# Attention feeding a feed-forward layer on one core: float16 operand parts under power-of-two scales in place of float32r parts

## The chip, the core and the metric

The kernel runs on one core of a Trainium2 chip. The metric is the device time of one execution in microseconds (us). Three timed runs of the kernel before gave 1097.66, 1099.0 and 1102.61 us: a median of 1099.0 us.

The core has five engines that each work through their own list of instructions in order: TensorE (PE, with its weight loads shown as PEld), VectorE (DVE), ScalarE (ACT), GpSimd (POOL) and SyncE (SP, which here issues the DMAs).

## What is computed

Random-feature attention over 8 batches and 8 heads (576 tokens, 64 dimensions, 128 features), and behind it a feed-forward layer on all 4608 tokens (512 to 2048 to 512, with a gelu). `setup_inputs` multiplies q by 4.675.

```python
def phi(x):                       # x = q * D**-0.25 or k * D**-0.25
    h = einsum('bhsd,md->bhsm', x, omega) - sum(x * x) / 2
    return exp(h - max(h)) / sqrt(m)
kv  = einsum('bhsm,bhsd->bhmd', phi(k), v);  z = sum(phi(k), axis=2)
out = einsum('bhsm,bhmd->bhsd', phi(q), kv) / (einsum('bhsm,bhm->bhs', phi(q), z) + 1e-06)
x   = out.transpose(0, 2, 1, 3).reshape(4608, 512)
h   = x @ w_in                    # 4608x512 @ 512x2048
g   = 0.5 * h * (1 + erf(h / sqrt(2)))
y   = g @ w_out                   # 4608x2048 @ 2048x512, float32
```

The two weight matrices arrive as float64; the kernel reads them as pairs of 32-bit words and makes float32 of them on the chip.

## The kernel before

**Attention** is cut into 32 units (a batch and a pair of heads). The first 4 units run ahead of everything else, in plain float32; the next 4 run in plain float32 beside the feed-forward work; the last 24 use split operands: a value is rounded to a high part, the rest is the low part, and the product is summed from high x high, high x low and low x high. A unit's result is written, transposed and divided, into tiles `xs[n, j]` of 128 x 384 values (`div`).

**The feed-forward layer** is cut into 12 blocks `n` of 384 tokens and 16 chunks `c` of 128 hidden columns. For each chunk `mm1` (L613) makes h from 4 pieces `j` of x and w_in, with 3 matmuls each (12 of 384 columns, L622); `act_high` (L624) applies the gelu to g and rounds it to `gh`; `act_low` (L633) makes `gl` = g - gh; `mm2` (L638) adds the chunk's share to the outputs of the block's three groups of 128 tokens, 3 matmuls each (9 of 512 columns, L645 to L647). All operands of these matmuls are float32r. `block_high` (L601) and `block_low` (L608) split a block's x in the same way on ACT and DVE (on POOL in block 0).

**Weights** come in 32 pieces of 128 x 512 (16 of w_in, 16 of w_out). For each, ACT scales the words (`w_scale`), DVE joins their bits (`w_bits`, L136 and L137), POOL adds the low word (`w_round`, L141), one of DVE, ACT or POOL rounds the high part (`w_high`, L148 to L152), and DVE (w_out) or POOL (w_in) subtracts for the low part (`w_low`, L155). A piece can go through all its steps as soon as it has landed.

**Order.** Every step is put into one list of events with a due time (`at(t, fn, ...)`, in steps of which a chunk of the feed-forward layer takes `SUB` = 6), the list is sorted, and the engines' instruction lists come from it; a scheduling layer below may still move instructions of one engine past each other. Attention units are spread over the feed-forward chunks by the list `bursts`. So PE's list interleaves chunks with attention matmuls, and an engine that waits holds all that stands behind it.

## Time and profile before

| | |
|---|---|
| timed runs | 1097.66, 1099.0, 1102.61 us (median 1099.0) |
| the profiled execution | 1100.79 us |
| its span, first to last instruction | 1098.9 us |
| mean granted TensorE clock | 0.992 |
| start to the first feed-forward matmul | 54.5 us |
| block 0 | 54.5 to 182.0 us |
| blocks 1 and 2 | 182.0 to 350.8 us |
| blocks 3 to 9 | 350.8 to 957.5 us |
| blocks 10 and 11 (no attention left) | 957.5 to 1098.9 us |

A block is counted from the first of its `mm1` matmuls to the first of the next block's. The span is what the profile covers, 1.9 us less than the execution's own time. In a row of the timeline the columns are the start in us, the duration in us, the engine, the line, the operation, the tiles (out<-in), the shape and how many were merged into the row; in square brackets stands an idle time before it and what ended it. In a group's row the numbers behind the bar are the busy time in us and the mean of one in ns, and then the idle time before them. The end of a matmul is modelled, and neighbours overlap; how fast matmuls follow each other is read from their starts. The rows themselves stand in the prediction.

### The profile page before, as it was taken

The page shows a single profiled execution, that of the slowest core. Times are in us where ns is not written, and L with a number is a line of the kernel's source. Part 1 is how long each engine was busy: PE and PEld are TensorE (multiplying, and loading weights), DVE is VectorE, ACT ScalarE, POOL GpSimd, SP SyncE. Part 2 cuts the span into 40 slices and gives each one's busy share as a digit, 9 for nine tenths or more (in the row PEclk, how much of TensorE's full clock was granted, in tenths as well). Part 3 has the DMA queues.
Part 4 walks back from the last instruction along what each step waited for, and adds up shares of the span by engine and source line. Part 5 has one row for each costly group of instructions (what it writes and reads, how often), then busy time and mean ns, then how long its engine had stood idle before and what let it go on. Part 6 is the DMA issues. An engine that isn't in the chain of part 4 may idle for free.

```text
span 1098.9 us, 17294 instructions
## 1 busy us (share of the span) xinstructions
PE 1049.1 (95%) x6022; PEld 906.3 (82%) x6022; DVE 789.7 (72%) x1780; ACT 618.0 (56%) x1310; POOL 482.4 (44%) x554
## 2 busy tenths in 40 slices
...
GB/s 232 169 110 150 164 117 60 70 44 44 75 44 56 84 56 52 62 50 47 72 56 56 75 32 56 57 62 55 56 74 41 49 63 1 1 29 1 30 1 30
DMA packets 46279, 70.92 MB, mean 65 GB/s; under 512 B 13680, under 2 KB 22256, under 8 KB 46192
## 3 DMA queue, kind: packets, MB, share of 16 engines
...
q14 instruction: 39, 0.32, 0.1%
...
## 4 chain that ended last, share of the span: by engine, by line
PE 64%; DVE 18%; ACT 2%; issue 2%; POOL 1%; POOLq 0%; ACTq 0%; DVEq 0%
PE h L622 27%; PE acc L647 9%; PE acc L646 9%; PE acc L645 9%; PE at L468 3%; PE at L400 3%; DVE gl L635 2%; DVE et L285 2%; PE at L249 2%; DVE mx L287 2%; PE at L277 1%; DVE xs L497 1%; DVE rt L485 1%; DVE rc L486 1%; DVE rt L488 1%
## 5 line engine op out<-in xcount | busy, mean ns | idle before, releaser
L622 PE MATMUL h<-xh,wih 128*128 128x384 f32 x768 | 263.2, 343 | 0.0
L622 PE MATMUL h<-xl,wih 128*128 128x384 f32 x768 | 262.5, 342 | 0.0
L622 PE MATMUL h<-xh,wil 128*128 128x384 f32 x768 | 262.0, 341 | 0.0
L645 PE MATMUL acc<-woh,gh 128*128 128x512 f32 (+1 forms) x576 | 230.8, 401 | 0.0
L647 PE MATMUL acc<-wol,gh 128*128 128x512 f32 (+1 forms) x576 | 226.6, 393 | 0.0
L646 PE MATMUL acc<-woh,gl 128*128 128x512 f32 (+1 forms) x576 | 226.2, 393 | 0.0
L635 DVE TENSOR_TENSOR gl<-g,gh 128x384 fp32r<-128x384 f32 x192 | 128.6, 670 | 121.1 <-ACT gh L630 120.6
L242 POOL TENSOR_TENSOR r<-xt,r 64x256 fp32r<-64x256 f32 (+2 forms) x216 | 173.8, 813 | 59.5 <-ACT r L236 46.4
L629 ACT ACTIVATE g<-h 128x384 f32<-128x384 f32 x192 | 94.4, 491 | 170.0 <-PE h L622 161.0
L373 POOL TENSOR_SCALAR kh<-et 128x256 f16<-128x256 f32 (+1 forms) x120 | 50.2, 425 | 280.8 <-ACT et L320 176.0
L622 PEld LDWEIGHTS h<-xh,wih 128*128 128x128 f32 x768 | 145.1, 189 | 7.7 <-issue 1.8
L622 PEld LDWEIGHTS h<-xh,wil 128*128 128x128 f32 x768 | 145.0, 189 | 6.3 <-issue 0.9
L622 PEld LDWEIGHTS h<-xl,wih 128*128 128x128 f32 x768 | 145.3, 189 | 1.3 <-issue 0.9
L647 PEld LDWEIGHTS acc<-wol,gh 128*128 128x128 f32 x576 | 108.3, 188 | 23.9
L645 PEld LDWEIGHTS acc<-woh,gh 128*128 128x128 f32 x576 | 108.5, 188 | 14.6 <-issue 1.5
L646 PEld LDWEIGHTS acc<-woh,gl 128*128 128x128 f32 x576 | 108.6, 189 | 12.8 <-issue 0.4
L236 ACT CAST r<-xt 128x256 fp32r<-128x256 f32 (+2 forms) x216 | 88.2, 410 | 51.9 <-PE at L277 44.2
L630 ACT CAST gh<-g 128x384 fp32r<-128x384 f32 x192 | 98.8, 515 | 3.3
L381 DVE SCALAR_TENSOR_TENSOR kl<-et,kh 128x256 f16<-128x256 f32 (+1 forms) x120 | 65.2, 559 | 30.7 <-POOL kh L373 28.9
L327 DVE STREAM_TRANSPOSE qt<-et 128x288 f32<-128x288 f32 x96 | 45.2, 471 | 51.8 <-ACT et L320 51.4
L141 POOL TENSOR_TENSOR wb<-wb,raw 128x512 int32<-128x512 int32 x32 | 44.0, 1376 | 67.5 <-DVE wb L137 30.3
L254 ACT COPY lo<-at 128x256 f32<-128x256 f32 (+1 forms) x120 | 41.9, 349 | 55.4 <-PE at L249 53.5
...
## 6 DMA issues: line engine op xcount, KB each, us to landing
...
```

Source lines behind the costliest of these rows:

```text
L236: nc.scalar.copy(u.r[i][:, 0:b - a], xf[:, a:b])
L242: nc.gpsimd.tensor_tensor(r, xf[D:, a:b], r, op=ALU.subtract)
L327: nc.vector.transpose(u.qt[g], ef[:, slice(*XG[NK + g])])
L373: nc.gpsimd.tensor_scalar(kh[:, :n], es, KSC, 1.0, op0=ALU.mult, op1=ALU.mult)
L381: nc.vector.scalar_tensor_tensor(kl[:, :n], es, KSC, kh[:, :n], op0=ALU.mult, op1=ALU.subtract)
L622: nc.tensor.matmul(h[:, 0:T], w, (xh, xh, xl)[k], start=(i == 0), stop=(i == 3 * NJ - 1))
L629: nc.scalar.activation(g, h[:, 0:T], AF.Gelu)
L630: nc.scalar.copy(gh, g)
L635: nc.vector.tensor_tensor(gl, g, gh, op=ALU.subtract)
L645: nc.tensor.matmul(acc, gh[:, s], woh[:, c, c0:c1], start=(c == 0), stop=False)
L646: nc.tensor.matmul(acc, gl[:, s], woh[:, c, c0:c1], start=False, stop=False)
L647: nc.tensor.matmul(acc, gh[:, s], wol[:, c, c0:c1], start=False, stop=(c == NF - 1))
```

## The change

- The four weight tiles are float16 in place of float32r. The joined float32 weights are kept for the whole run in a new tile, `w32`.
- **A scale for each weight matrix, found on the chip.** When a piece has been joined, DVE takes its largest absolute value (`w_max`). When all 16 pieces of a matrix have one, a *chain* of small steps makes a scale of them: DVE takes the maximum over the pieces (`chain_a`), PE transposes the 128 values (`chain_b`), DVE takes their maximum (`chain_c`), PE spreads it over the partitions by a matmul with ones (`chain_d`), DVE keeps the exponent bits (`chain_e`), and POOL makes from them a power of two and its inverse (`chain_f`, three instructions). Only then can `w_high` and `w_low` run: so they are put behind the chains, for w_in from due time 72 and for w_out from 91, within block 0, and no longer piece by piece. `w_high` is on POOL and ACT in turn, `w_low` on DVE for all 32 pieces.
- **A scale for each block of x** from block 1 on, by the same chain: four maxima of 128 x 384 on DVE (`block_max`), the chain, and three more POOL instructions (`block_scales`); `block_high`, `block_low`, the gelu, `gh`, `gl` and the output copy then take scales as per-partition operands.
- **Block 0** uses plain float32 for both products (`mm1_first`, and a branch in `mm2`): one matmul in place of three, from `w32`, `xs` and g themselves. It has no `block_high`, `block_low`, `gh` or `gl`.
- Buffers: `xs` 11 in place of 9, g 3 in place of 1, `xh` and `xl` 8 in place of 4, and the output tile has its own 2.
- The attention units of the split kind start at due time 112 with 33.4 between them (8 of them), then 36, in place of 115 and 35; the last one starts at 922 in place of 920.

The diff, with the unchanged lines cut:

```diff
--- before.py
+++ after.py
...
+TOP = 13
...
-    wih = cp.tile([P, NJ, F], F32R, name="wih")
-    wil = cp.tile([P, NJ, F], F32R, name="wil")
-    woh = cp.tile([P, NF, DM], F32R, name="woh")
-    wol = cp.tile([P, NF, DM], F32R, name="wol")
+    wih = cp.tile([P, NJ, F], F16, name="wih")
+    wil = cp.tile([P, NJ, F], F16, name="wil")
+    woh = cp.tile([P, NF, DM], F16, name="woh")
+    wol = cp.tile([P, NF, DM], F16, name="wol")
+    w32 = cp.tile([P, 2, NF, 512], I32, name="w32")
+    wmax = cp.tile([P, 2, NF], F32, name="wmax")
+    wsc = cp.tile([P, 2, 3], F32, name="wsc")
...
     def w_round(pc):
...
+    def w_max(pc):
+        nc.vector.tensor_reduce(wmax[:, pc.win, pc.i:pc.i + 1], pc.w, axis=AX.X, op=ALU.max, apply_absolute_value=True)
...
     def w_high(pc):
-        pc.w = pc.b.bitcast(F32)
-        if pc.win:
-            pc.w = pc.w.rearrange("p (j w) -> p j w", j=NJ)
-        if pc.e[0] is nc.gpsimd:
-            nc.gpsimd.tensor_scalar(pc.wh, pc.w, 1.0, 1.0, op0=ALU.mult, op1=ALU.mult)
-        elif pc.e[0] is nc.vector:
-            nc.vector.tensor_copy(pc.wh, pc.w)
+        need(('wsc', pc.win))
+        s = wsc[:, pc.win, 1:2]
+        w = pc.w.rearrange("p (j w) -> p j w", j=NJ) if pc.win else pc.w
+        if pc.i % 2:
+            nc.scalar.activation(pc.wh, w, AF.Copy, scale=s)
...
-            nc.scalar.copy(pc.wh, pc.w)
+            nc.gpsimd.tensor_scalar(pc.wh, w, s, 1.0, op0=ALU.mult, op1=ALU.mult)
...
     def w_low(pc):
-        pc.e[1].tensor_tensor(pc.wl, pc.w, pc.wh, op=ALU.subtract)
+        s = wsc[:, pc.win, 1:2]
+        w = pc.w.rearrange("p (j w) -> p j w", j=NJ) if pc.win else pc.w
+        nc.vector.scalar_tensor_tensor(pc.wl, w, s, pc.wh, op0=ALU.mult, op1=ALU.subtract)
...
+    def chain_a(c):
+        c.c = sp.tile([P, 1], F32, tag="cm", name="cm", bufs=2)
+        nc.vector.tensor_reduce(c.c, c.m, axis=AX.X, op=ALU.max)
+    def chain_b(c):
+        c.ps = ps_at()
+        nc.tensor.transpose(c.ps[0:1, 0:P], c.c, ident)
+    def chain_c(c):
+        c.t = sp.tile([1, 1], F32, tag="ct", name="ct", bufs=2)
+        nc.vector.tensor_reduce(c.t, c.ps[0:1, 0:P], axis=AX.X, op=ALU.max)
+    def chain_d(c):
+        nc.tensor.matmul(c.ps[:, P:P + 1], ones, c.t, start=True, stop=True)
+    def chain_e(c):
+        e = c.sc[:, 0:1].bitcast(I32)
+        nc.vector.tensor_scalar(e, c.ps[:, P:P + 1].bitcast(I32), 0x7f800000, None, op0=ALU.bitwise_and)
+    def chain_f(c):
+        nc.gpsimd.tensor_scalar(e, e, 187 * one, 87 * one, op0=ALU.min, op1=ALU.max)
+        nc.gpsimd.tensor_scalar(s, e, -1.0, (254 + TOP) * one, op0=ALU.mult, op1=ALU.add)
+        nc.gpsimd.tensor_scalar(r, e, 1.0, -TOP * one, op0=ALU.mult, op1=ALU.add)
+    def chain_events(c, t, dt):
+        for k, f in enumerate((chain_a, chain_b, chain_c, chain_d, chain_e, chain_f)):
+            at(t + k * dt, f, c)
...
-            xs[n, j] = sp.tile([P, T], F32, tag="xs", name=f"xs{n}_{j}", bufs=9)
+            xs[n, j] = sp.tile([P, T], F32, tag="xs", name=f"xs{n}_{j}", bufs=11)
...
+    def block_max(n, j):
+        if j == 0:
+            bsc[n] = (sp.tile([P, NJ], F32, tag="xm", name="xm", bufs=2), sp.tile([P, 6], F32, tag="bs", name="bs", bufs=3))
+        nc.vector.tensor_reduce(bsc[n][0][:, j:j + 1], xs[n, j], axis=AX.X, op=ALU.max, apply_absolute_value=True)
+    def block_chain(f, n):
+        f(chains[n])
+    def block_scales(n):
+        z = float(DM) * 2.0 ** (2 * TOP + 2 - 15)
+        nc.gpsimd.tensor_tensor(b[:, 3:4], b[:, 2:3], wsc[:, 1, 2:3], op=ALU.mult)
+        nc.gpsimd.tensor_scalar(b[:, 4:5], b[:, 1:2], wsc[:, 1, 1:2], 1.0 / z, op0=ALU.mult, op1=ALU.mult)
+        nc.gpsimd.tensor_scalar(b[:, 5:6], b[:, 3:4], z, 1.0, op0=ALU.mult, op1=ALU.mult)
     def block_high(n, j):
-        xh = mp[0].tile([P, T], F32R, tag="xh", name="xh", bufs=4)
-        xl = mp[0].tile([P, T], F32R, tag="xl", name="xl", bufs=4)
-        nc.scalar.copy(xh, xs[n, j])
+        need(('bs', n))
+        xh = mp[0].tile([P, T], F16, tag="xh", name="xh", bufs=8)
+        xl = mp[0].tile([P, T], F16, tag="xl", name="xl", bufs=8)
+        nc.scalar.activation(xh, xs[n, j], AF.Copy, scale=bsc[n][1][:, 1:2])
...
     def block_low(n, j):
...
-        (nc.gpsimd if n == 0 else nc.vector).tensor_tensor(xl, xs.pop((n, j)), xh, op=ALU.subtract)
+        nc.vector.scalar_tensor_tensor(xl, xs.pop((n, j)), bsc[n][1][:, 1:2], xh, op0=ALU.mult, op1=ALU.subtract)
...
+    def mm1_first(c, p):
+        if p == 0:
+            hs[0, c] = ps_h()
+        for j in ((0, 1), (2,), (3,))[p]:
+            nc.tensor.matmul(hs[0, c][:, 0:T], wi32[:, c, j], xs[0, j], start=(j == 0), stop=(j == NJ - 1))
     def mm1(n, c, p):
+        if n == 0:
+            return mm1_first(c, p)
...
     def act_high(n, c):
...
-        g = mp[0].tile([P, T], F32, tag="g", name="g", bufs=1)
-        gh = mp[0].tile([P, T], F32R, tag="gh", name="gh", bufs=3)
-        gl = mp[0].tile([P, T], F32R, tag="gl", name="gl", bufs=3)
-        nc.scalar.activation(g, h[:, 0:T], AF.Gelu)
-        nc.scalar.copy(gh, g)
+        g = mp[0].tile([P, T], F32, tag="g", name="g", bufs=3)
+        if n == 0:
+            nc.scalar.activation(g, h[:, 0:T], AF.Gelu)
+            gs[n, c] = g
+            return
+        gh = mp[0].tile([P, T], F16, tag="gh", name="gh", bufs=3)
+        gl = mp[0].tile([P, T], F16, tag="gl", name="gl", bufs=3)
+        nc.scalar.activation(g, h[:, 0:T], AF.Gelu, scale=bsc[n][1][:, 3:4])
+        nc.scalar.activation(gh, g, AF.Copy, scale=bsc[n][1][:, 4:5])
...
     def act_low(n, c):
...
-        nc.vector.tensor_tensor(gl, g, gh, op=ALU.subtract)
+        nc.vector.scalar_tensor_tensor(gl, g, bsc[n][1][:, 4:5], gh, op0=ALU.mult, op1=ALU.subtract)
...
     def mm2(n, c, i, c0=0, c1=DM):
-        need(('w', False, c), ('g', n, c))
+        need(('g', n, c))
...
+        if n == 0:
+            nc.tensor.matmul(acc, gs[n, c][:, s], w32f[:, 0, c], start=(c == 0), stop=(c == NF - 1))
+            return
+        need(('w', False, c))
...
     def store(n, i, c0=0, c1=DM):
...
-            os[0] = mp[0].tile([P, DM], F32, tag="raw", name="o", bufs=3)
+            os[0] = mp[0].tile([P, DM], F32, tag="o", name="o", bufs=2)
...
-        nc.vector.tensor_copy(o, accs.pop((n, i, c0))[:, 0:c1 - c0])
+        acc = accs.pop((n, i, c0))[:, 0:c1 - c0]
+        if n == 0:
+            nc.vector.tensor_copy(o, acc)
+        else:
+            nc.vector.tensor_scalar(o, acc, bsc[n][1][:, 5:6], wsc[:, 0, 2:3], op0=ALU.mult, op1=ALU.mult)
...
+    at(BASE - 3, nc.vector.memset, ones, 1.0)
-    bursts = [5 + 20.5 * k for k in range(NJ)] + [115 + 35 * k for k in range(len(units) - 2 * NJ)]
+    bursts = [5 + 20.5 * k for k in range(NJ)]
+    bursts += [112 + 33.4 * k if k < 8 else 346 + 36 * (k - 7) for k in range(len(units) - 2 * NJ)]
...
-        for j in range(NJ):
-            t = n * NF * SUB - (5, 4, 3, 3)[j]
-            at(t, block_high, n, j)
-            at(t + 0.6, block_low, n, j)
+        t = n * NF * SUB - (9 if n == 1 else 15)
+        if n:
+            for j in range(NJ):
+                at(t + 0.2 * j, block_max, n, j)
+                at(t + 5 + 0.7 * j, block_high, n, j)
+                at(t + 5.6 + 0.7 * j, block_low, n, j)
+            for k, f in enumerate((chain_a, chain_b, chain_c, chain_d, chain_e, chain_f)):
+                at(t + 1 + 0.6 * k, block_chain, f, n)
+            at(t + 4.7, block_scales, n)
...
-            at(t + 4.5, act_low, n, c)
+            if n:
+                at(t + 4.5, act_low, n, c)
...
```

Three places of the instruction lists, as the two programs have them. A name such as `w_71` or `xs_1_419` is a tile with its number; `x9` at the end of a row stands for nine such instructions in a row.

PE, a chunk's first product in block 0, before: twelve float32r matmuls with the three pairs of parts of each piece (one loop, of which these are the first six).

```order
L622 MATMUL h<-xh,wih 128x384
L622 MATMUL h<-xh,wil 128x384
L622 MATMUL h<-xl,wih 128x384
L622 MATMUL h<-xh,wih 128x384
L622 MATMUL h<-xh,wil 128x384
L622 MATMUL h<-xl,wih 128x384
```

PE, the same product in the changed kernel, just behind the chain of w_in late in block 0 (L196 is the chain's transpose, L203 its matmul with ones, L736 block 0's second product, L621 an attention unit's product).

```order
L196 MATMUL at<-ident,cm 1x128
L736 MATMUL acc<-w_71,g 128x512
L203 MATMUL at<-ct,ones 128x1
L736 MATMUL acc<-w_71,g 128x512 x2
L621 MATMUL at<-et,v 65x128 x10
L693 MATMUL h<-xs_0_281,w_71 128x384
L693 MATMUL h<-xs_1_419,w_71 128x384
L693 MATMUL h<-xs_2_557,w_71 128x384
L693 MATMUL h<-xs_3_658,w_71 128x384
```

Twelve matmuls have become four of another kind, and two small matmuls stand in PE's list that each wait for a maximum on DVE, with one matmul of block 0 between them.

DVE, the low parts of the weights, before: one at a time, between the steps of pieces and of attention.

```order
L136 TENSOR_SCALAR wb<-raw 128x512
L155 TENSOR_TENSOR wol<-wb,woh 128x512
L137 SCALAR_TENSOR_TENSOR wb<-raw,wb 128x512
L594 TENSOR_REDUCE nm<-at 128x4 x2
L596 TENSOR_TENSOR et<-at,nm 128x512 x2
L150 CAST wih<-wb 128x4x128
```

DVE in the changed kernel, behind the chain of w_in (L200 is the chain's second maximum, L208 its exponent bits, L170 a low part, L535 to L538 and L544 an attention unit's division, L636 and L637 the next unit's small copies).

```order
L200 TENSOR_REDUCE ct<-at 1x1
L536 TENSOR_SCALAR rc<-rt 128x9
L537 RECIPROCAL rc<-rc 128x9
L208 TENSOR_SCALAR wsc<-at 128x1
L538 STREAM_TRANSPOSE rt<-rc 128x288
L544 TENSOR_TENSOR xs_2_1316<-at,rt 128x288
L170 SCALAR_TENSOR_TENSOR wil<-w_71,wsc,wih 128x4x128 x9
L636 COPY kvz<-at 128x2x64
L637 COPY kvz<-at 128x2x64
L170 SCALAR_TENSOR_TENSOR wil<-w_71,wsc,wih 128x4x128 x7
L658 TENSOR_REDUCE xm<-xs_2_1316 128x1
```

All sixteen low parts of w_in now stand together on DVE, with two small copies between them; those of w_out follow, six ahead of block 1's first `gl` and ten behind it.

PE, a block's chain further on (block 2's, in block 1's last chunks; L740 to L742 are the second product, L706 the first). Each float16 matmul now has a weight load of its own in the list.

```order
L196 MATMUL at<-ident,cm 1x128
L740 LDWEIGHTS gh
L740 MATMUL acc<-woh,gh 128x512
L741 LDWEIGHTS gl
L741 MATMUL acc<-woh,gl 128x512
L742 LDWEIGHTS gh
L742 MATMUL acc<-wol,gh 128x512
L203 MATMUL at<-ct,ones 128x1
L706 LDWEIGHTS wih
L706 MATMUL h<-xh,wih 128x384
```

Between the two small matmuls of the chain stand three matmuls of the second product; DVE's small maximum has to be made in that time.

62 lines of the change are left out of this document (44 added, 18 removed).

## The prediction

> **What bounds the kernel now.** I read the page's busy shares and the chain of waits first, then busy time by stage, then the spacing of matmuls.
>
> ```profile
> span 1098.9 us, 17294 instructions
> PE 1049.1 (95%) x6022; PEld 906.3 (82%) x6022; DVE 789.7 (72%) x1780; ACT 618.0 (56%) x1310; POOL 482.4 (44%) x554
> PE 64%; DVE 18%; ACT 2%; issue 2%; POOL 1%; POOLq 0%; ACTq 0%; DVEq 0%
> ```
>
> PE carries the chain, DVE is second in both rows. By stage (start; block 0; blocks 1 and 2; 3 to 9; 10 and 11; the columns are the stage, its length, then the busy time of PE, PEld, DVE, ACT and POOL, the granted clock, DMA):
>
> ```profile
> 0.00:54.50 54.50, 46.50 (x379) 34.39 (x379) 39.38 (x104) 42.50 (x123) 31.70 (x34) 0.97 0.68 202
> 54.50:182.00 127.50, 111.45 (x668) 88.81 (x668) 103.15 (x205) 78.42 (x137) 58.61 (x52) 0.95 0.41 124
> 182.00:350.80 168.80, 166.45 (x939) 145.84 (x938) 135.90 (x317) 102.28 (x219) 89.86 (x107) 1.00 0.20 59
> 350.80:957.50 606.70, 586.37 (x3303) 510.60 (x3302) 485.54 (x1111) 360.69 (x766) 302.24 (x363) 1.00 0.18 52
> 957.50:1098.90 141.40, 138.29 (x739) 126.71 (x737) 25.78 (x46) 34.09 (x68) 0.00 (x0) 1.00 0.05 17
> ```
>
> From block 1 on PE is busy over 96% of the time, with DVE at 80% (485.54 of 606.70) while attention runs. In block 0 PE is idle for 16 us (127.5 - 111.45) and DVE is busy 81%. So the end is set by PE's matmul rate, and by DVE's lateness in block 0.
>
> **The matmul rate.** PE's timeline in block 11, where nothing waits (start, duration):
>
> ```profile
> 1040.31 0.28 PE L645 MATMUL acc<-woh,gh 128*128 128x256 f32 x1
> ...
> 1041.02 0.34 PE L622 MATMUL h<-xh,wih 128*128 128x384 f32 x1
> ...
> 1043.12 0.39 PE L645 MATMUL acc<-woh,gh 128*128 128x512 f32 x1
> ...
> 1044.51 0.28 PE L645 MATMUL acc<-woh,gh 128*128 128x256 f32 x1
> ```
>
> Between the first two rows lie 6 matmuls of 256 columns, then 12 of 384 and 6 of 512: 0.118, 0.175 and 0.232 us each. A chunk takes 12 x 0.175 + 9 x 0.232 = 4.19 us, a block 67 us, and blocks 10 and 11 are little else. For two-byte operands there are the 22 warm-up matmuls at the start (ends of the run of equal ones, by two windows) and an attention product, float16 against bfloat16:
>
> ```profile
> 4.33 0.82 PE L506 MATMUL h<-z 128*128 128x256 bf16 x6
> 4.66 0.49 PE L506 MATMUL h<-z 128*128 128x256 bf16 x3
> ...
> 515.38 0.23 PE L400 MATMUL at<-vb,kl 128*128 128x129 bf16 x1
> 515.44 0.25 PE L400 MATMUL at<-vb,kh 128*128 128x193 bf16 x1
> 515.53 0.22 PE L400 MATMUL at<-vb,kl 128*128 128x129 bf16 x1
> 515.59 0.24 PE L400 MATMUL at<-vb,kh 128*128 128x193 bf16 x1
> 515.61 0.48 PE L645 MATMUL acc<-woh,gh 128*128 128x512 f32 x1
> 515.93 0.39 PE L646 MATMUL acc<-woh,gl 128*128 128x512 f32 x1
> ```
>
> Three more warm-up matmuls add 0.33 us: 0.11 us for 256 columns; with the last digit 0.42 to 0.44 ns per column, against float32r's 0.118 / 256 = 0.46. The short attention matmuls go at 0.21 us for 129 + 193 + 129 columns, 0.466 ns: no better than float32r, but they are hardly longer than a weight load. The feed-forward matmuls (384, 512) are nearer to the warm-up. and longer, which makes a fixed part of each weigh less: I take 0.425, so 0.163 and 0.218, a chunk of 12 x 0.163 + 9 x 0.218 = 3.92 us, **0.27 us less**, over 176 chunks (blocks 1 to 11) **-48 us**. Bounds: nothing (the attention rows) and -56 (0.42). Every float16 matmul needs its own weight load in the list; the attention rows already have one each, 0.06 to 0.09 us apart, so it hides.
>
> One rule speaks against this. The Trainium skill, TensorE: Matmul & The Clock Gate, section Weight-path perf modes, says that the array handles one element per cell and cycle whatever the element's width, and its section Back-to-back issue gap has one formula for all types. By it the first term would be nothing; the 0.118 against 0.11 at 256 columns disagrees.
>
> **Block 0 in float32.** A plain float32 matmul shows as two records; attention has them with 128 columns:
>
> ```profile
> 9.63 1.09 PE L571 MATMUL acc<-et,v 128*65 128x128 f32 x8
> ...
> 19.48 2.40 PE L571 MATMUL h<-et,v 128*65 128x128 f32 x20
> ```
>
> Twelve more records add 1.31 us, 0.109 each: 1.71 ns per column of a matmul. A chunk is then 4 x 384 x 1.71 + 3 x 512 x 1.71 ns = 5.25 us, 1.06 more than before: **+17 us** of PE work in block 0. PE's 16 idle us are waits for DVE there, so some of the 17 may fill them (waits of PE in block 0: total, times, longest):
>
> ```profile
> PE at L439 <- DVE et L596: 9.1, 3, 5.1
> PE at L459 <- DVE et L596: 2.8, 4, 0.9
> PE at L533 <- DVE xs L494: 2.6, 2, 1.9
> ```
>
> What DVE does decides:
>
> ```profile
> L635 DVE TENSOR_TENSOR gl<-g,gh 128x384 fp32r<-128x384 f32 x192 | 128.6, 670 | 121.1 <-ACT gh L630 120.6
> L155 DVE TENSOR_TENSOR wol<-wb,woh 128x512 fp32r<-128x512 f32 x16 | 14.9, 928 | 9.8 <-POOL woh L148 8.1 <-ACT woh L152 1.2
> L261 DVE TENSOR_REDUCE nm<-et 128x2 f32<-128x256 f32 x96 | 39.3, 409 | 1.3
> L594 DVE TENSOR_REDUCE nm<-at 128x4 f32<-128x512 f32 x16 | 10.4, 679 | 3.3 <-PE at L533 3.2
> L150 DVE CAST wih<-wb 128x512 fp32r<-128x512 f32 x8 | 4.9, 615 | 2.7 <-POOL wb L141 2.7
> L487 DVE RECIPROCAL rc<-rc 128x9 f32<-128x9 f32 x64 | 12.6, 197 | 0.8
> ```
>
> Removed by the start of block 1: 16 `gl` (10.7), 16 low parts (14.9), 8 casts (4.9): 30.5 us. Added by then: 32 maxima at 0.68 (21.7), 22 low parts at 0.93 (20.4), 7 maxima of 384 columns at 0.54, halfway between 0.41 and 0.68 (3.8), three chains of three small steps at 0.2 (1.8): 47.7 us. That is **+17 us** of DVE work on 39.38 + 103.15. Two engines get 17 us more each in a stretch of 182 us with 24 us of idle PE time; POOL loses 16 low parts of w_in and the four `xl` of block 0, which stood ahead of its first matmul. I take **+9 us** for start and block 0; bounds: 0, if the idle time takes all of it, and +25, if DVE's and half of PE's add up.
>
> **Blocks 1 and 2.** -8.7 of the first term (32 chunks). DVE gets ten low parts of w_out (9.3) and in each block four maxima and a chain (2.8 each): 15 us, and about 4 more since the attention units start 33.4 apart: 135.90 + 19 = 155 of 168.8, 92%. The highest share shown is block 0's 81%, with PE waiting. So the gain is likely eaten: **0**, bounds -7 (all hidden) and +13 (DVE's 155 at block 0's 81% would need 191, at 85% 182; 182 is 13 over 168.8).
>
> **What each block pays.** The scale chain sends two small matmuls through PE, each waiting for DVE. The nearest thing is the q maximum of a unit, also a transpose behind a DVE reduction:
>
> ```profile
> 602.32 0.40 PE L645 MATMUL acc<-woh,gh 128*128 128x512 f32 x1
> 603.24 0.29 PE L293 MATMUL at<-ident,mx 128*36 128x128 f32 x1 [0.52 <-DVE mx L287]
> 603.28 0.47 PE L646 MATMUL acc<-woh,gl 128*128 128x512 f32 x1
> ...
> L293 PE MATMUL at<-ident,mx 128*36 128x128 f32 x24 | 6.8, 284 | 4.7 <-DVE mx L287 4.5
> L303 PE MATMUL at<-ident,sm 36*128 36x36 f32 x24 | 6.0, 249 | 0.3
> ```
>
> Here the matmuls around it are 0.96 us apart instead of 0.23; on the mean the idle time is 4.7 / 24 = 0.2 us. I take 0.7 us for a block's chain with its two steps (0.3 to 1.5). It gates `xh` and `xl` of the next block, due ten steps (some 9 us) before they are used, so POOL's six small steps and ACT's four hide there. Then the change of type: where a float32r matmul follows a float16 one (515.59 to 515.93) the two starts are 0.34 apart, against 0.09 + 0.23: 0.02 to 0.03 lost. Before, only the 120 groups of L400 did that; now nearly every float32r piece of attention among feed-forward matmuls does, some 20 times in a block by the changed list: +0.5 us a block. DVE has 2.8 us more work per block in a stage where it is 80% busy and PE is 3% idle: +0.5.
>
> `gl` and `xl` with a scale are one DVE instruction as before. L381 is such a one and shows no surcharge:
>
> ```profile
> L381 DVE SCALAR_TENSOR_TENSOR kl<-et,kh x120: 244/427/1020, 199.4 to 935.1; 128x256 f16<-128x256 f32 x96, 128x128 f16<-128x128 f32 x24
> L635 DVE TENSOR_TENSOR gl<-g,gh x192: 508/557/2157, 70.1 to 1090.6; 128x384 fp32r<-128x384 f32 x192
> ```
>
> Medians 0.427 for 256 and 0.557 for 384 lie on one line of 1.02 ns per column: nothing there. Three buffers for g instead of one let ACT run ahead; PE doesn't wait for g now, so nothing.
>
> **Sum.** Blocks 3 to 9: 112 x -0.27 = -30.2, chains +4.9, changes of type +3.5, DVE +3.5: **-18** (bounds -31 and +5). Blocks 10 and 11: 32 x -0.27 + 0.7: **-8** (-10 to 0). With +9 and 0 that is **-17 us**. The profiled execution took 1100.8 us, 1.9 more than its span and 1.8 over the median: 1083.8 there, **1082 us** in timed runs.
>
> **Rivals.**
> - *The additions are hidden*: block 0's idle time takes the float32 work, the chains find DVE ahead. For it: in blocks 3 to 9 DVE waits 120.6 us in all for `gh`, so it often runs ahead. Then start and block 0 +3, blocks 1 and 2 -7, blocks 3 to 9 -28 (the changes of type stay), the end -9: -41, 1058.
> - *DVE sets the end of the first three blocks*: place, the sixteen low parts of w_in in one row and those of w_out behind, ahead of the division and maxima that PE's attention matmuls and chains wait for; price, block 0 +25, blocks 1 and 2 +13, against -14 (DVE's waits twice as dear) and -8: +16, 1115. It decides once DVE is over about 90% busy there. For it: 92% worked out above. Against: the low parts are 22 x 0.93 in a stretch where PE has 17 us more of its own.
> - *The matmuls don't get faster*: the rows of 0.466 ns. Then 1082 + 48 = 1130. By the rule of the Trainium skill quoted above the result would be this one. Against: the warm-up rows.
> - *A draw*: the chains cost 1.5 and DVE's waits grow 1.5 a block; -17 + 11 x 0.8 + 9 x 1 = +1: 1100.
>
> **How the numbers follow.** Forecast 0.50 (own range 1070 to 1092), additions hidden 0.19, DVE 0.11, no faster matmuls 0.04, draw 0.16. The range reaches from near the hidden case to short of DVE's: 1060 to 1103. A measurement here can tell about 0.5% (5.5 us) from no change. Faster than 1093.5: the forecast, the hidden case and a little of the draw, 0.71. Within 0.5%: most of the draw, 0.15. Slower: 0.14.
>
> **What would show it.** In blocks 10 and 11, float16 matmuls 0.163 and 0.218 apart right, 0.175 and 0.232 wrong. Block 0's first-product records 0.32 us apart (0.64 a matmul). Block 1 starts near 191 us; later than 200 speaks for DVE, with PE's waits put down to DVE's division, L646 or L170. PE's idle time before L196 and L203 near 0.3 each. Blocks 3 to 9 near 589 us. Wrong would be a stage that I don't have: PE waiting for ACT or POOL (the scales), or weight loads of float16 that show.

## The result and the profile after

The change makes the kernel 1.2% slower: a median of 1112.17 us in four timed runs (1110.31 to 1114.97) against 1099.33 for the kernel before in the same rounds (1097.66 to 1102.61). The ratio is 1.0115, with a 95% interval from 1.0082 to 1.0149. The forecast was 1082. The page of the changed kernel, the rows that answer to the first three quoted of before:

```profile
span 1108.5 us, 17209 instructions
PE 1031.4 (93%) x5949; PEld 604.4 (55%) x5949; DVE 829.7 (75%) x1888; ACT 650.4 (59%) x1298; POOL 472.7 (43%) x606
PE 40%; DVE 31%; ACT 8%; issue 4%; POOL 4%; DMA 1%; POOLq 0%; DVEq 0%; ACTq 0%
```

PE is busy 17.7 us less, and yet the span is 9.6 us longer. The chain that ended last was 64% PE and 18% DVE; it is 40% PE, 31% DVE and 8% ACT. By the same stages (start; block 0; blocks 1 and 2; 3 to 9; 10 and 11):

```profile
0.00:50.30 50.30, 45.20 (x378) 34.69 (x378) 38.28 (x109) 40.28 (x118) 12.62 (x15) 0.97 0.76 209
50.30:193.40 143.10, 128.03 (x572) 69.94 (x572) 115.53 (x235) 78.10 (x130) 58.20 (x62) 0.95 0.40 114
193.40:371.50 178.10, 165.35 (x950) 96.16 (x949) 154.64 (x343) 113.67 (x227) 95.88 (x123) 0.99 0.20 55
371.50:975.60 604.10, 563.41 (x3312) 331.31 (x3311) 491.57 (x1156) 378.08 (x759) 304.63 (x402) 0.99 0.19 53
975.60:1108.50 132.90, 129.45 (x742) 72.33 (x740) 29.67 (x49) 40.28 (x68) 1.40 (x6) 1.00 0.05 18
```

| stage | before | after | difference | forecast |
|---|---|---|---|---|
| start and block 0 | 182.0 | 193.4 | +11.4 | +9 |
| blocks 1 and 2 | 168.8 | 178.1 | +9.3 | 0 |
| blocks 3 to 9 | 606.7 | 604.1 | -2.6 | -18 |
| blocks 10 and 11 | 141.4 | 132.9 | -8.5 | -8 |

Two stages came out near the forecast. In the other two some 25 us are missing. In blocks 3 to 9 PE's busy time fell by 23 us (586.37 to 563.41), but its time between matmuls doubled (20.3 us not busy before, 40.7 now).

**The matmuls are as fast as forecast.** PE's timeline in block 11:

```profile
1049.74 0.27 PE L741 MATMUL acc<-woh,gl 128*128 128x256 f16 x1
...
1050.29 0.33 PE L706 MATMUL h<-xh,wih 128*128 128x384 f16 x1
...
1052.24 0.38 PE L740 MATMUL acc<-woh,gh 128*128 128x512 f16 x1
...
1053.53 0.27 PE L740 MATMUL acc<-woh,gh 128*128 128x256 f16 x1
```

Between these rows lie 5 matmuls of 256 columns, 12 of 384 and 6 of 512: 0.110, 0.1625 and 0.215 us each, where 0.163 and 0.218 were forecast for the last two. A chunk takes 12 x 0.1625 + 9 x 0.215 = 3.89 us, against 4.19 before; the rival of matmuls that don't get faster falls. The weight loads do not show.

**The instructions that take a scale are longer.** Groups of the changed kernel (busy us, mean ns | idle before):

```profile
L724 DVE SCALAR_TENSOR_TENSOR gl<-g,bs,gh 128x384 f16<-128x384 f32 x176 | 127.2, 729 | 129.3 <-ACT gh L719 128.7
L719 ACT ACTIVATE gh<-g,bs 128x384 f16<-128x384 f32 x176 | 106.6, 614 | 2.8
L718 ACT ACTIVATE g<-h,bs 128x384 f32<-128x384 f32 x176 | 101.7, 579 | 153.9 <-PE h L706 152.7
L679 ACT ACTIVATE xh<-xs,bs 128x384 f16<-128x384 f32 x44 | 25.4, 606 | 19.5 <-POOL bs L214 19.5
L684 DVE SCALAR_TENSOR_TENSOR xl<-xs,bs,xh 128x384 f16<-128x384 f32 x44 | 31.3, 728 | 8.8 <-ACT xh L679 8.7
```

The first three with the scale as an immediate (an experiment, below):

```profile
L723 DVE SCALAR_TENSOR_TENSOR gl<-g,gh 128x384 f16<-128x384 f32 x176 | 124.6, 708 | 110.5 <-ACT gh L718 110.1
L718 ACT ACTIVATE gh<-g 128x384 f16<-128x384 f32 x176 | 92.2, 525 | 2.8
L717 ACT ACTIVATE g<-h 128x384 f32<-128x384 f32 x176 | 86.2, 490 | 162.0 <-PE h L705 160.7
```

and shortest, median and longest `gl` in ns, of the changed kernel:

```profile
L724 DVE SCALAR_TENSOR_TENSOR gl<-g,bs,gh x176: 570/619/1720, 198.7 to 1100.5; 128x384 f16<-128x384 f32 x176
```

and with the immediate:

```profile
L723 DVE SCALAR_TENSOR_TENSOR gl<-g,gh x176: 539/559/1732, 200.1 to 1076.2; 128x384 f16<-128x384 f32 x176
```

ACT's gelu and `gh` are 0.089 us longer each, DVE's `gl` 0.060 by the medians. That is 0.24 us more on the way of each chunk from h to `gl`.

**A place where it is lost.** The largest stalls of PE after block 0 are two of 4.17 us, in blocks 4 and 7. POOL, ACT, DVE and PE around the first (start, duration; in brackets the idle time before, and what ended it):

```profile
538.57 0.19 POOL L214 TENSOR_SCALAR bs<-bs 128x1 int32<-128x1 int32 x1
538.80 1.12 ACT L679 ACTIVATE xh<-xs,bs 128x384 f16<-128x384 f32 x2 [3.06 <-POOL bs L214]
539.45 0.62 DVE L684 SCALAR_TENSOR_TENSOR xl<-xs,bs,xh 128x384 f16<-128x384 f32 x1 [3.13 <-ACT xh L679]
541.25 2.99 DVE L684 SCALAR_TENSOR_TENSOR xl<-xs,bs,xh 128x384 f16<-128x384 f32 x2
541.42 2.41 POOL L316 TENSOR_TENSOR et<-et,nm 128x1152 f32<-128x1152 f32 x1 [0.23 <-DVE nm L311]
544.17 1.14 DVE L724 SCALAR_TENSOR_TENSOR gl<-g,bs,gh 128x384 f16<-128x384 f32 x1
546.30 0.17 DVE L537 RECIPROCAL rc<-rc 128x9 f32<-128x9 f32 x1
546.52 0.52 PE L327 MATMUL at<-r,om 128*128 128x288 f32 x2 [4.17 <-DVE rc L537]
546.86 0.52 PE L706 MATMUL h<-xl,wih 128*128 128x384 f16 x1
547.17 0.53 PE L706 MATMUL h<-xh,wih 128*128 128x384 f16 x1
```

Read downwards: POOL reaches the scale only behind its attention pieces; ACT has stood 3.06 us for it, DVE 3.13 us for ACT's `xh`; two `xl` then take 2.99 us where two alone take 1.2, while POOL runs a piece of 2.41 us; the division (`rc`), for which PE waits, stands behind all that in DVE's list. Behind the stall PE's next matmuls start 0.31 us apart instead of 0.1625: the granted clock is 0.50 from 546.87 to 550.28 us. The Trainium skill (TensorE: Matmul & The Clock Gate, "Why this matters for your kernels") advises against idle gaps of PE over about 3 us, since its clock is then halved; the two gaps of 4.17 us agree. Shorter gaps can have the same effect here, and not every time: in `e17_scales_on_dve` (below) PE stands for 1.89 us up to 730.70 us, and the granted clock is 0.50 from 731.90 on; in the changed kernel it stands for 1.89 us ahead of the same attention matmul, up to 732.71 us, and the clock stays at 1.00.

Blocks 1 to 9 of the changed kernel hold three stretches of 3.41 us at half clock (from 226.02, 546.87 and 806.29 us); blocks 1 to 9 of the kernel before hold none. At half speed that is at most 5 of the 25 us that are missing. The forecast had no term for it.

### The profile page after: what moved, and what is told of

Its sections match the earlier page's. It is cut to its first block, busy times and chain, and to the rows that moved or that the text cites. A ratio compares the mean times of both kernels' runs of the same rounds, so it can differ in the third digit from the quotient of the medians.

```text
span 1108.5 us, 17209 instructions
## 1 busy us (share of the span) xinstructions
PE 1031.4 (93%) x5949; PEld 604.4 (55%) x5949; DVE 829.7 (75%) x1888; ACT 650.4 (59%) x1298; POOL 472.7 (43%) x606
## 4 chain that ended last, share of the span: by engine, by line
PE 40%; DVE 31%; ACT 8%; issue 4%; POOL 4%; DMA 1%; POOLq 0%; DVEq 0%; ACTq 0%
PE h L706 17%; PE acc L742 5%; PE acc L741 5%; PE acc L740 5%; DVE gl L724 5%; DVE et L335 3%; DVE mx L337 2%; DVE ql L386 2%; DVE kl L431 2%; ACT gh L719 2%; ACT et L370 2%; DVE wil L170 1%; DVE rt L535 1%; PE at L450 1%; ACT g L718 1%
## 5 line engine op out<-in xcount | busy, mean ns | idle before, releaser
L706 PE MATMUL h<-xl,wih 128*128 128x384 f16 x704 | 230.8, 328 | 0.0
L706 PE MATMUL h<-xh,wih 128*128 128x384 f16 x704 | 230.7, 328 | 0.0
L706 PE MATMUL h<-xh,wil 128*128 128x384 f16 x704 | 230.3, 327 | 0.0
L724 DVE SCALAR_TENSOR_TENSOR gl<-g,bs,gh 128x384 f16<-128x384 f32 x176 | 127.2, 729 | 129.3 <-ACT gh L719 128.7
L740 PE MATMUL acc<-woh,gh 128*128 128x512 f16 x528 | 200.2, 379 | 1.8 <-DVE o L753 1.8
L741 PE MATMUL acc<-woh,gl 128*128 128x512 f16 x528 | 199.1, 377 | 0.0
L742 PE MATMUL acc<-wol,gh 128*128 128x512 f16 x528 | 199.0, 377 | 0.0
L706 PEld LDWEIGHTS <-wih 128*128 128x128 f16 x1408 | 134.3, 98 | 83.5 <-issue 0.6
L719 ACT ACTIVATE gh<-g,bs 128x384 f16<-128x384 f32 x176 | 106.6, 614 | 2.8
L706 PEld LDWEIGHTS <-wil 128*128 128x128 f16 x704 | 69.1, 98 | 42.6 <-issue 0.7
L742 PEld LDWEIGHTS <-gh 128*128 128x128 f16 x544 | 53.4, 98 | 59.1 <-issue 0.8
L740 PEld LDWEIGHTS <-gh 128*128 128x128 f16 x544 | 53.2, 98 | 41.8 <-issue 0.6
L299 PE MATMUL at<-om,r 128*128 128x256 f32 x216 | 63.6, 366 | 7.8 <-DVE kvz L467 7.7
```

The costliest lines, as they stand in the source:

```text
L299: nc.tensor.matmul(u.pp[i][:, t], r[:, t * P:(t + 1) * P], om, start=True, stop=True)
L706: nc.tensor.matmul(h[:, 0:T], w, (xh, xh, xl)[k], start=(i == 0), stop=(i == 3 * NJ - 1))
L719: nc.scalar.activation(gh, g, AF.Copy, scale=bsc[n][1][:, 4:5])
L724: nc.vector.scalar_tensor_tensor(gl, g, bsc[n][1][:, 4:5], gh, op0=ALU.mult, op1=ALU.subtract)
L740: nc.tensor.matmul(acc, gh[:, s], woh[:, c, c0:c1], start=(c == 0), stop=False)
L741: nc.tensor.matmul(acc, gl[:, s], woh[:, c, c0:c1], start=False, stop=False)
```

## The experiments

A scale of x that fits all blocks of this data, with those of the weights, can be written into the instructions as constants. That allows each part of the change to be taken away alone. Four theories stood at the start: **A**, the loss comes from finding the scales, by operands and by the chain; **B** and **C**, by one of these alone; **D**, by the changed distances of the attention units (33.4 and 36 steps in place of 35).

### Chain and scale operands, apart and together

Constants in a tile, no chain (`e2_const`): the four `block_max`, the chain and `block_scales` are not called, and

```diff
-    bsc, chains = {}, {}
+    cb = cp.tile([P, 6], F32, name="cb")
+    bsc, chains = {n: (None, cb) for n in range(NBLK)}, {}
...
+        for c, e in enumerate((0, 19, 0, -35, 13, -13)):
+            nc.vector.memset(cb[:, c:c + 1], 2.0 ** e)
...
```

> Left out: the maxima of x and the chain of each block (four DVE maxima, two small matmuls, three DVE and POOL steps and the POOL products); a block's six scales stand in a tile of constants, filled once, that fit this data, and every ACT and DVE instruction still takes its scale from that tile, one value per partition. The weights' maxima and chains stay. Theory A (the loss of blocks 1 to 9, 46 us more than before over the bare matmul time, comes from finding the scales: partly from the scale operands, which lengthen gelu, gh and gl by 0.06 to 0.1 us each, partly from the chain, whose POOL step makes ACT's xh wait 19.5 us in all and DVE's xl 8.7 us): 1090 us, halfway, and the 4.2 us PE stalls ahead of two of the blocks are gone. Rival B (the chain and its waits alone): 1075 us, like the kernel with immediate scales. Rival C (the scale operands alone): 1105 us. Rival D (the attention units 33.4 and 36 apart instead of 35): 1112 us, the stalls stay.

Immediates, no chain (`e3_imm`); the scales of `xh`, `xl` and the output copy are replaced in the same way:

```diff
...
-        nc.scalar.activation(g, h[:, 0:T], AF.Gelu, scale=bsc[n][1][:, 3:4])
-        nc.scalar.activation(gh, g, AF.Copy, scale=bsc[n][1][:, 4:5])
+        nc.scalar.activation(g, h[:, 0:T], AF.Gelu, scale=2.0 ** -35)
+        nc.scalar.activation(gh, g, AF.Copy, scale=2.0 ** 13)
...
-        nc.vector.scalar_tensor_tensor(gl, g, bsc[n][1][:, 4:5], gh, op0=ALU.mult, op1=ALU.subtract)
+        nc.vector.scalar_tensor_tensor(gl, g, 2.0 ** 13, gh, op0=ALU.mult, op1=ALU.subtract)
```

> Left out: as in the kernel with constants, the maxima and the chain of each block; and the block scales are now immediates in the instructions (powers of two that fit this data), no operand. The weights' maxima and chains, block 0 in float32, the attention's spacing and the places of the instructions stay as in the change. Theory A: 1072 us (1060 to 1085): both halves of the scale finding are gone, gelu, gh and gl go back to about 0.49, 0.52 and 0.56 us. Rival B: 1075, the same as with constants. Rival C: 1080, well under the kernel with constants. Rival D (attention spacing): 1105 or more, since the spacing is kept. If the loss is in the changed block 0 and the bunched low parts, start to block 3 stays at 371 us and the rest falls by no more than 10 us.

Immediates, with the whole chain running unused (`e4_chain_idle`):

> Nothing is left out of the scale finding's work: maxima, chain and POOL products of each block run as in the change; but their result is unused, and the instructions take immediates that fit this data. So no ACT or DVE instruction waits for a scale and none has a scale operand. Theory A: 1085 us (1078 to 1095), about 12 over the kernel without the chain: 44 maxima at 0.54 us, 33 small DVE steps and 22 small matmuls. Rival B with the work as the cause: 1110, the change's time. Rival B with the wait as the cause: 1075. Rival C: 1080. Rival D: 1105 or more.

| | scales as immediates | scale operands |
|---|---|---|
| no chain | 1084.3 (ratio 0.982 to 0.989) | 1090.2 (0.988 to 0.994) |
| chain | 1101.9, unused (1.000 to 1.005) | 1112.2, the change (1.008 to 1.015) |

The ranges are the 95% intervals of the ratio to before. The chain's work costs 17.6 us, the operands 5.9 without the chain and, with the wait for its result, 10.3 beside it. Theory A holds against B and C, and D does not explain the 28 us between 1084.3 and 1112.2, since all four kernels have the new distances. Its 1090 for constants in a tile came out, but its other sizes were off: 1084 for 1072 (other losses stay), 1102 for 1085 (the chain is dearer).

Part of the operands' price goes with the granted clock. `e2_const` took 1085.0 and 1086.3 us in its two executions at a mean clock of 0.994 to 0.995, and 1089.7 to 1094.5 in the four at 0.987 to 0.989; the kernel with immediates took 1084.1 to 1084.4 at 0.994 to 0.995. At the same clock the operands alone cost 1 to 2 us, not 5.9; whether they bring the lower clock about is not shown. The chain's price stays: unused, it took 1099.6 and 1099.8 us at 0.994 to 0.995, 15 us more than none. The operands beside the chain keep a price too: at 0.986 to 0.989 the change took 1110.3 to 1115.0, the unused chain 1104.0 and 1105.5.

### What of the chain costs

Maxima alone (`e7_max_idle`), then the chain alone on a column of constants (`e8_chain_only`), both with immediates:

> The kernel with immediate block scales (1084.3 us) with the 44 block maxima (four of 384 columns in each block, 0.54 us each on DVE) put back, their result unused; no chain. Left out: the chain; the scales are constants that fit this data. With maxima and chain, unused, it was 1101.9. Theory A1 (DVE's time decides: 24 us of maxima, of which what blocks 1 to 9 hold lies on PE's path about half): 1095 us (1091 to 1099). Rival A2 (the chain's steps back and forth between DVE, PE and POOL decide, the maxima lie in DVE's waits): 1087 or less.

> The kernel with immediate block scales (1084.3 us) with each block's chain put back (three small DVE steps, a transpose and a small matmul on PE, six POOL steps), run on a column of constants; its result is unused. Left out: the 44 block maxima; the scales are constants that fit this data. Theory A1 (DVE's time decides): 33 small steps of 0.15 to 0.27 us are 6 us, and PE's two waits a block at 0.7 as predicted 7: 1091 us (1088 to 1094). Rival A2 (the chain decides): 1098 or more, with PE's idle time at the transpose and the small matmul over 1 us a block.

Measured 1092.8 (ratio 0.991 to 0.996) and 1092.7 (0.992 to 0.996): 8.5 us each over 1084.3, and together about what both cost (17.6). So each block pays 0.77 us for four maxima (2.2 us of DVE work) and 0.77 for its chain, as A1 has it. PE's idle time at the two small matmuls of the changed kernel stays small:

```profile
L203 PE MATMUL at<-ct,ones 1*128 1x1 f32 x26 | 4.9, 256 | 1.2 <-DVE ct L200 1.1
L196 PE MATMUL at<-ident,cm 128*1 128x128 f32 x13 | 3.5, 271 | 3.1 <-DVE xs L544 2.0 <-DVE et L335 0.6 <-DVE et L310 0.4
L658 DVE TENSOR_REDUCE xm<-xs 128x1 f32<-128x384 f32 x44 | 23.6, 539 | 0.4
```

### Float16 parts alone

The kernel before with float16 tiles and fixed scales (`e6_f16_alone`; the weights' 2^16 is folded into the factor that they are unpacked with):

```diff
-    wih = cp.tile([P, NJ, F], F32R, name="wih")
...
+    wih = cp.tile([P, NJ, F], F16, name="wih")
...
-        nc.scalar.activation(hf, hf, AF.Copy, scale=2.0 ** -112)
+        nc.scalar.activation(hf, hf, AF.Copy, scale=2.0 ** -110)
...
-        nc.vector.tensor_tensor(gl, g, gh, op=ALU.subtract)
+        nc.vector.scalar_tensor_tensor(gl, g, 2.0 ** 13, gh, op0=ALU.mult, op1=ALU.subtract)
...
```

> The kernel before with one thing changed: the feed-forward parts are float16 instead of float32r, under fixed powers of two as immediates (x 2^19, both weights 2^16, folded into the factor that their unpacking has already, gelu's input 2^-35, gh and gl 2^13, the output 2^-29). No maxima, no chain, block 0 in parts as before (its four xl on DVE), weights' parts made piece by piece as before, the attention's spacing as before. The matmul rate alone is worth 192 chunks x 0.27 = 52 us: theory A says 1099 - 52 + 5 for changes of type and DVE = 1052 us (1045 to 1065). Rival (DVE and ACT already hold PE in blocks 3 to 9, so that a faster PE only waits more): 1075 to 1085. Rival (float16 weight loads or changes of type cost what the rate gains): 1095 or more.

Measured 1062.8 us, ratio 0.966 (0.963 to 0.970): the fastest kernel of this study, with scales that fit this data and are not found on the chip. Its blocks 1 and 2, 3 to 9, and 10 and 11:

```profile
177.90:341.40 163.50, 157.81 (x938) 93.88 (x937) 136.80 (x317) 101.86 (x220) 89.89 (x107) 1.00 0.22 61
341.40:930.00 588.60, 556.83 (x3304) 328.52 (x3303) 486.92 (x1112) 359.75 (x766) 301.54 (x363) 1.00 0.19 54
930.00:1061.80 131.80, 128.71 (x739) 72.09 (x737) 25.85 (x47) 34.28 (x68) 0.00 (x0) 1.00 0.05 19
```

Where no attention runs the stage gains 9.6 us, all of 32 x 0.30 (4.19 to 3.89 us a chunk). In blocks 3 to 9 the matmul rate is worth 30 us by the forecast's 0.27, and PE's busy time falls by 29.5 (586.37 to 556.83), but the stage is only 18 us shorter: PE is not busy for 31.8 us instead of 20.3, nearly all of it waits for DVE.

### Block 0, the weights' parts and the attention's distances

`e5_imm_old_times` is the kernel with immediates with the distances of before and `xh` and `xl` at their old places; `e5c_imm_new_bursts_old_x` has only the latter; `e9b_pieces_old_times` is `e5_imm_old_times` with the weights' parts made piece by piece as before, so that beside float16 only block 0 in float32 and some buffer counts are left of the change.

The distances, and in `e9b_pieces_old_times` also `w_high` and `w_low` right behind `w_round`:

```diff
...
-            at(t, w_high, pc)
-            at(t + 1, w_low, pc)
...
+        w_events(po, 5.5 * i, (-7, 0, 1, 2, 3, 4))
...
-    bursts = [5 + 20.5 * k for k in range(NJ)]
-    bursts += [112 + 33.4 * k if k < 8 else 346 + 36 * (k - 7) for k in range(len(units) - 2 * NJ)]
+    bursts = [5 + 20.5 * k for k in range(NJ)] + [115 + 35 * k for k in range(len(units) - 2 * NJ)]
...
```

> The kernel with immediate block scales and without the blocks' maxima and chains (1084.3 us), with the attention units again at the kernel before's distances (35 throughout, from 115 on) and each block's xh and xl again at their places before (5 to 3 steps ahead of the block). Left out: the blocks' maxima and chains; the scales are constants that fit this data. Theory A (the spacing is no cause): 1084 us, 4 either way. Rival D (the spacing is a cause of the loss): 1075 or less. That the new spacing is what makes room for the weights' work behind block 0: 1092 or more.

> The kernel with immediate block scales (1084.3 us), with the attention units at the change's distances (33.4, then 36), and only each block's xh and xl back at their places before (5 to 3 steps ahead of the block). With both back it was 1078.0. Left out: the blocks' maxima and chains; the scales are constants that fit this data. Rival D (the distances of the attention units are the 6 us): 1084. The places of xh and xl, 10 steps earlier, and no distance: 1078.

> The kernel with immediate block scales at the kernel before's distances, and beside that the weights' parts made piece by piece as before: each piece's high and low part right behind its unpacking, on the engines of before (w_in's low parts on POOL). Left out: the blocks' and the weights' maxima and chains; all scales are constants that fit this data. What stays of the change beside float16 is block 0 in plain float32 and the buffers of g and o. Theory E (the 32 weight maxima and the 32 low parts in a row on DVE are what costs blocks 1 and 2 the 12.5 us by which the kernel with immediates is behind float16 alone): 1072 us (1068 to 1076), 9 over float16 alone (1062.8) for block 0 in float32. Rival F (block 0 in float32 alone: 17 us of PE work): 1080 us. Rival: block 0 in float32 hides in DVE's waits: 1064.

Measured 1078.0 (ratio 0.978 to 0.983), 1084.8 (0.985 to 0.989) and 1083.4 (0.983 to 0.988). So the distances cost 6.8 us (1084.8 less 1078.0), D in part; the places of `xh` and `xl` cost nothing. Theory E fell: made piece by piece the parts are 5.4 us *dearer* than in a row with maxima and two chains. Rival F is the nearest: over float16 alone, block 0 in float32 (with the buffer counts, which were not taken alone) costs 20.6, where F had 17. The size of the float32 work can be read in the changed kernel's timeline:

```profile
183.14 1.45 PE L693 MATMUL h<-xs,w 128*128 128x384 f32 x4
186.73 0.81 PE L693 MATMUL h<-xs,w 128*128 128x384 f32 x2
195.65 1.02 PE L736 MATMUL acc<-w,g 128*128 128x512 f32 x2
198.10 1.88 PE L736 MATMUL acc<-w,g 128*128 128x512 f32 x4
```

Two more records add 0.64 and 0.86 us: 4 x 0.64 + 3 x 0.86 = 5.14 us a chunk against 3.89 in float16, 16 x 1.25 = 20 us. Little of it hid: start and block 0 together are 21.5 us longer than with float16 alone (199.4 against 177.9), and PE's idle time in them falls by 3.3 us only (26.6 to 23.3).

The clock is mixed into these two prices. In start and block 0 of the profiled executions the mean granted clock is 0.91 in `e9b_pieces_old_times`, 0.95 with float16 alone and 0.98 in `e5_imm_old_times`; counted as time lost that is some 17, 9 and 3 us. So of the 5.4 us and of the 20.6 us a part that is not known is a lower clock, and why these kernels differ in it stays open.

### Which use of the scales costs

The change with immediates for the gelu, `gh`, `gl` and `o`, so that only `xh` and `xl` use the chain's result (`e10_wait_only`); with immediates on DVE alone (`e11_act_operands`); with immediates on ACT alone (`e12_dve_operands`). The chain finds one of two neighbouring powers of two for x in this data, the immediates stand for one of them; in the other blocks the parts of these three kernels do not fit together, and only their time is used.

> The change, with the scales of gelu, gh, gl and o as immediates that fit this data; xh and xl (8 instructions a block) still take x's scale from the block's chain and wait for it. Nothing is left out of the chain. The change is 1112.2, the kernel with chain and nothing that uses it 1101.9. Theory A (the operands of the instructions on each chunk are what those 10 us are): 1103 (1100 to 1106). Rival (the wait of ACT and DVE for POOL's scale, 19.5 and 8.7 us in the change, is what they are): 1110.

> The change, with the scales of DVE's gl, xl and o as immediates that fit this data; ACT's xh, gelu and gh keep their scale operands, with the chain's result. Theory A: gelu and gh are 0.16 us longer on the way of each chunk, gl 0.06, so most of the 10 us stay with ACT: 1109 (1106 to 1111). Rival (DVE is the nearer engine to the end, so gl's 0.06 us, 176 times, decide): 1105 or less.

> The change, with the scales of ACT's xh, gelu and gh as immediates that fit this data; DVE's gl, xl and o keep their scale operands, with the chain's result. Theory A (ACT's operands decide): 1105 (1103 to 1108). Rival (DVE's operands decide): 1109 or more.

Measured 1097.5 (0.997 to 0.9995), 1123.5 (1.021 to 1.025) and 1107.7 (1.006 to 1.009). Without operands on each chunk the change takes 14.7 us less, below theory A's range, although ACT still waits as long for POOL:

```profile
L679 ACT ACTIVATE xh<-xs,bs 128x384 f16<-128x384 f32 x44 | 25.1, 605 | 20.7 <-POOL bs L214 20.7
```

So these operands are what costs, not the wait by itself. But the prices do not add up: `e10_wait_only` does more than `e4_chain_idle` and is 4.4 us faster; ACT's operands alone make 26 us over `e10_wait_only`, DVE's alone 10, both together 14.7 (these two also lack an operand that `e10_wait_only` has, on `xl` or on `xh`). The run with ACT's alone contradicts both theories. Its blocks 4 and 7 have a stall of 3.2 us where `e10_wait_only` has 2.5 or less, and PE waits for `kl` 19 times for 10.6 us, against 3.0 there; in blocks 3 to 9 its clock is halved for four stretches of 3.41 us, against two in the change, which is 3.4 us at most. The rest of the 11 us by which it lies above the full change is not explained.

### DVE's place of gl

`gl` two steps later in the order: in the change (`e13_after_gl_65`), in the kernel with operands on ACT alone (`e16_act_gl_65`), with float16 alone (`e14_f16_gl_65`) and in the kernel before (`e15_before_gl_65`).

```diff
-                at(t + 4.5, act_low, n, c)
+                at(t + (4.5 if n == NBLK - 1 else 6.5), act_low, n, c)
```

> The change with one thing else: DVE's gl of each chunk stands two steps later in the order (6.5 instead of 4.5 after the chunk's first matmul; the last block as it was), so that DVE does the attention steps that stood behind it first. Nothing is left out. Theory G (what the scale operands and the added work cost is paid where DVE stands at gl for ACT's gh, 128.7 us in all in the change, while attention steps that PE waits for are queued behind it): 1098 (1090 to 1104). Rival: PE's second product then waits for gl, 1115 or more. Rival: DVE's load, not its order, decides: 1112.

> The kernel with scale operands on ACT alone (1123.5 us) with gl two steps later, as above; the immediates on DVE stand for one of the two scales that the chain finds in this data, so in the other blocks the parts don't fit together and only the time is read. Theory G: its 11 us over the change are DVE's longer stand at gl for gh (132.3 us, against 108.3 where ACT has immediates); they go, and it comes to within 4 us of the change with gl two steps later. Rival: the operands on ACT cost it elsewhere: the 11 us stay.

> Float16 parts alone (1062.8 us; the kernel before with fixed scales, block 0 in parts) with gl two steps later. Theory G: float16 gave 18 us in blocks 3 to 9 where the matmul rate alone gives 30, since PE waits more for DVE there; with DVE not standing at gl the rest comes in part: 1055 (1048 to 1060). Rival: no change, 1063.

> The kernel before (1099 us) with gl two steps later. Theory G: PE waits less for DVE there (20 us idle in blocks 3 to 9): 1094 (1088 to 1098). Rival: no change, since at float32r's rate DVE's stand at gl is covered: 1099.

Measured 1112.4, 1120.6, 1064.0 and 1100.3: no difference in three and 3 us in one, `e16_act_gl_65` (as above, only its time is used). The edit did not do what it was for: between 350 and 950 us of the change DVE's wait for `gh` was 30.9 us and is 30.2. Theory G started from 128.7 us of that wait, but only 37.2 of them lie in blocks 3 to 9; most of the rest is in blocks 10 and 11, where no attention stands behind it. Theory G found no support, but was not tested cleanly.

### POOL's steps on DVE

The six small scale steps of a chain on DVE instead of POOL, in the change (`e17_scales_on_dve`) and in the kernel with operands on ACT alone (`e18_act_scales_on_dve`):

```diff
-        nc.gpsimd.tensor_scalar(e, e, 187 * one, 87 * one, op0=ALU.min, op1=ALU.max)
...
+        nc.vector.tensor_scalar(e, e, 187 * one, 87 * one, op0=ALU.min, op1=ALU.max)
...
```

> The change with the six small scale steps of each chain (L213 to L215, L670 to L672) on DVE instead of POOL, at the same places in the order. Nothing is left out. Theory H (the stalls of 4.2 us ahead of blocks 5 and 8 begin where POOL's scale steps stand behind its attention pieces: ACT's xh waits 3.1 us for POOL, DVE's xl 3.1 us for xh, and DVE's division, for which PE waits, stands behind xl): the two stalls go, ACT's 19.5 us of waiting for POOL too, 11 x 6 x 0.15 us of DVE work come: 1104 (1098 to 1108). Rival (the waits for POOL are covered, what counts is the length of the instructions on each chunk): 1112 to 1116.

> The kernel with scale operands on ACT alone (1123.5 us; the immediates on DVE stand for one of the two scales that the chain finds in this data, so only its time is read), with the six scale steps on DVE as above. Theory H: its excess over the change comes from the same places, so it falls by more than the change does, to 1108 or less. Rival: the excess is the length of ACT's instructions and stays: 1120 or more.

Measured 1106.0 (ratio 1.004 to 1.008) and 1114.9 (1.012 to 1.018): 6.2 and 8.5 us less. The first is within theory H's range, the second between H's value and its rival's. Waits of `e17_scales_on_dve` from 190 to 980 us (total, times, longest):

```profile
ACT xh L679 <- DVE bs L214: 4.5, 5, 3.5
DVE xl L684 <- ACT xh L679: 1.0, 3, 0.5
```

The same of the changed kernel:

```profile
ACT xh L679 <- POOL bs L214: 17.5, 8, 3.1
DVE xl L684 <- ACT xh L679: 7.5, 5, 3.1
```

And the place of the stall in `e17_scales_on_dve`:

```profile
539.75 2.35 POOL L316 TENSOR_TENSOR et<-et,nm 128x1152 f32<-128x1152 f32 x1 [1.48 <-ACT r L286]
540.06 2.46 DVE L724 SCALAR_TENSOR_TENSOR gl<-g,bs,gh 128x384 f16<-128x384 f32 x1
544.48 0.82 PE L327 MATMUL at<-r,om 128*128 128x288 f32 x2 [3.63 <-DVE rc L536]
```

ACT's wait for the scale is gone for the most part (17.5 to 4.5 us), DVE's behind it too (7.5 to 1.0), and with them 6 us. Half of theory H fell: the stall is still 3.6 us. Now it is a `gl` that takes 2.46 us while POOL runs its 2.35 us piece. So the stall has a second half, the place where POOL's long piece meets a DVE instruction. The excess of the kernel with operands on ACT alone stays at 9 us.

## Why the prediction was wrong, step by step

The sum from the experiments, each rung a median: before 1099.3; float16 alone 1062.8 (-36.5); block 0 in float32 1083.4 (+20.6); the weights' maxima and parts in a row 1078.0 (-5.4); the attention's distances 1084.3 (+6.3); the chain's work 1101.9 (+17.6); its use 1112.2 (+10.3). The prices were measured in this order and would differ by some microseconds in another; the kernel before itself varied by 1.0 us between these measurements, and the rungs of block 0 and of the weights' parts hold differences of the granted clock, as said above. For the stages:

- **The matmul rate** (-0.27 us a chunk): right, to 0.003 us a matmul. **That it comes out in full in blocks 3 to 9**: wrong. The forecast took 30 us less 3.5 for changes of type; the kernel with immediates, which has no chain, gains 22 (606.7 to 584.6). What is missing went to PE's waits for DVE, which the prediction priced at the added work only and not at the faster PE.
- **"L381 is such a one and shows no surcharge"**: the step that failed most. L381 has an immediate, and for that form it was right (0.559 us with an immediate against 0.557 for the subtraction before, medians of `gl`); that L381 and L635 lie on one line showed nothing, since two points always do. The new `gl`, `xl`, gelu, `gh` and `xh` have an operand for each partition, and ACT's part of this did not enter the sum at all. It is +60 ns on DVE's `gl` by the medians and +89 ns on ACT. In blocks 3 to 9 operands and wait are worth 9 us (604.1 against 595.2 with the chain unused), where the sum had 0. Both kernels have two stretches of half clock in this stage.
- **The chain and DVE's 2.8 us more a block** (4.9 + 3.5 in blocks 3 to 9): the sizes were nearly right. In this stage the maxima alone add 3.8 us (588.4 against 584.6, where +3.5 was forecast for DVE) and the chain alone 5.5 (590.1, where +4.9 was); both together add 10.6 (595.2), of which two stretches of half clock are up to 3.4. How the chain costs it is only partly as forecast: PE's idle time at its two small matmuls is 4.3 us for 13 chains, 0.33 each, where 0.7 stood for each chain.
- **"POOL's six small steps and ACT's four hide there"**: wrong. ACT waited 19.5 us for POOL's, and taking them off POOL gained 6.2 us. Yet in `e10_wait_only` ACT waits as long (20.7 us) and the kernel is no slower than with the chain unused; so the price of this wait depends on the rest of the kernel.
- **Changes of type** (+3.5, from 0.02 to 0.03 us each): hardly seen. Where two float32r matmuls of attention (256 columns, L249 before, L299 now) stand between feed-forward matmuls with no idle time, the median time from the start of the feed-forward matmul before them to that of the one behind them went from 0.407 to 0.4045 us for 384 columns and from 0.468 to 0.453 for 512 (counted from all records in blocks 1 to 9). The feed-forward matmul alone became 0.0125 and 0.017 us shorter, so at most 0.01 us is lost for a pair.
- **Blocks 1 and 2** (0): 178.1 is 9.3 over 168.8. The range of -7 to +13 held it, the value did not. DVE's 154.64 us were forecast as 155, and PE waited for them. By the rungs' traces: float16 -5.3, block 0's float32 +2.4, the weights' parts in a row +3.8, the distances +6.4, chain and operands +2.0. The distances, the largest, had entered the sum as DVE work alone.
- **Start and block 0** (+9): +11.4, near in number, but by luck as the sum of terms that the prediction had otherwise. Block 0's float32 (5.14 against 4.19 us a chunk, 15 us) came almost whole, where PE's idle time was to take much of it; and with the weights' parts behind block 0 the kernels with immediates got 10 us shorter there (199.4 to 189.1), where the prediction had DVE's later work as a cost. In these 10 us is the difference of the granted clock (0.91 to 0.98), so the two are not told apart.
- **The end** (-8): -8.5, right.
- **The rival of hidden additions** was given 120.6 us of DVE's waiting for `gh` "in blocks 3 to 9" as its support. That is the wait of the whole run: 11.7 us of it lie in blocks 3 to 9 and 102.3 in blocks 10 and 11. DVE had little time to spare where attention runs.

In all, -17 was forecast for the span and +9.6 came: blocks 1 and 2 have 9.3 of the 26.6, blocks 3 to 9 15.4, start and end 1.9. The rival of DVE in the first three blocks had a time of 1115, near the result by chance, for its places were others: block 0 took +11 and not +25, and the loss lay in blocks 3 to 9 above all. The sentence on what would be wrong named "PE waiting for ACT or POOL (the scales)"; it came as PE waiting for DVE, with ACT and POOL ahead of DVE.
